# Fused linear attention and gated FFN: seven block products for tiles 8 and 9 of the down projection, tile 10 in their banks, and no forced query unit

## The chip, the cores and the metric

The kernel runs on one core of one Trainium2 chip. The metric is the device time of one execution in microseconds (us), the median of several runs. PE is the matmul engine (TensorE), DVE, ACT and POOL are VectorE, ScalarE and GpSimd, SP is the engine whose queue issues nearly all of the DMAs.

## The reference

```python
xn = layernorm(x)                            # x: 2048 x 512
q, k, v = heads(xn @ wqkv)                   # 32 heads of 16
phi_q = [softmax(q @ w_phi), softmax(-(q @ w_phi))]      # phi_k the same way
kv, z = phi_k.T @ v, phi_k.sum(tokens)       # per head
o = (phi_q @ kv) / (phi_q @ z + 1e-6)
s = o @ wo
h = relu(xn @ W_gate) * (xn @ W_up)          # 2048 x 1376
out = x + s * silu(h @ W_down)
```

All is float32.

## The kernel before

**Precision.** Each operand is split into a high part (rounded for the fast matmul) and a low part (the remainder). A product is three matmuls into one bank: low weight x high data, high weight x low data, high x high (`mm3`, or `mm` three times). A split is a copy to the high part on ACT and a subtraction on POOL or DVE for the low part (`split`). Names: hh, hl are the high and low part of the FFN's hidden values, fdh, fdl of the down weights of a tile, wth, wtl of a weight block that is loaded for a block product, XT slots are reused for operands of block products.

**Tiling.** Tokens are 4 blocks of 512. Half 0 is blocks 0 and 1 (b0, b1), half 1 is blocks 2 and 3. The 1376 hidden features are 11 tiles of 128, of which the last is part full. For each tile `gate_up` makes gate and up of both blocks of a half by a seven-product scheme in four banks pa, pb, pc, pd; it is a generator that yields between products, and other work (the down products of earlier tiles, query projections) is put in at the yields. Its last two steps finish the hidden values of b1 (t7) and b0 (r).

**The down projection.** In half 0 tiles go in chunks, and the chunk (8, 9, 10) comes after the last `gate_up`: b1's products, then b0's, each ended by a Silu. In half 1, the down products of tiles 0 to 3 (group 0) and 4 to 7 (group 1) are made transposed (features on partitions) as 7 block products in place of 8. `operand_parts` makes the sums of hidden values on POOL and splits them, `weight_sums` makes those of the down weights on POOL and puts them into DRAM tiles wdt{g}{i}{h,l} (group g, product i), `weights` loads them back as wth, wtl, and `turned_down(g)` issues the matmuls, product i in the order of ORDER, two tiles t each, two feature tiles k deep. Products 1, 2 and 4 take a weight block as it is. The products of one bank are added up there, and DVE adds the bank to y. Tiles 8, 9 and 10 (REST_F) are made plainly in `last_turned`, 2 blocks x 4 columns of 128 x 3 tiles x 3 matmuls. Then comes `out_turned` (pso: the attention output times wo, 12 matmuls a bank, times y, plus x) for two pairs of query tiles, and the last ones in `out_tile`.

**Queries.** The features of queries are made in units of two (`q_pair`: exponentials, row sums, normalization eq), and `q_back` is a unit's back part: DVE transposes eq to ez, 32 small matmuls (pnum) multiply it with the key-value state, and ACT copies the numerators out, to be stored to DRAM (od). They are read back as `of` and split to oh, ol for pso.

**What sets the order.** All operations are recorded in the order in which the program issues them (`InOrder`, so that nearly all have one line in the profile: L75), and each engine keeps that order. The program order itself comes from a planner: the class `Clock` holds rough costs, and at each `pump` a background generator goes on as soon as its inputs are there by that clock and its engine's backlog is within a limit; `finish` runs one to its end at once. `weight_sums`, `weights`, `operand_parts` and the queries are such generators. SP's queue issues its DMAs in order.

Of the kernel before, what the change touches and what calls it, by code (L numbers as in the profile page):

```python
# [8 lines left out]
F32R = mybir.dt.float32r  # L9
AF = mybir.ActivationFunctionType  # L10
ALU = mybir.AluOpType
# [38 lines left out]

GROUPS = [(0, 1, 2, 3), (4, 5, 6, 7)]
IN_GROUP = {f: (g, m // 2, m % 2) for g, fs in enumerate(GROUPS) for m, f in enumerate(fs)}
ORDER = (5, 3, 1, 6, 7, 2, 4)
PLAIN = {1: (0, 0), 2: (0, 1), 4: (1, 1)}
# [121 lines left out]
def layer_kernel(ctx: ExitStack, tc: tile.TileContext, x, wkT, wqT, wv, wo, wf, cst, out):  # L176
# [539 lines left out]
    def d_load(g):  # L716
        RD[g] = [u4((P, 2, D), "rd") for h in range(2)]
        for m, f in enumerate(GROUPS[g]):
            nc.sync.dma_start(RD[g][m // 2][:, m % 2, :], wf[f][:, 1024:])

    WDT = {(g, i): [dram((P, 512), f"wdt{g}{i}{x}") for x in "hl"] for g in range(len(GROUPS)) for i in (5, 6, 3, 7)}

    def weight_sums():

        for g in range(len(GROUPS)):
            if g not in RD:
                yield 100,
                d_load(g)
            a11, a21, a12, a22 = (halves(t)[:, x] for t in RD.pop(g) for x in range(2))
            yield 40,  # L730
            yield "sync", a11, a22
            t = u2((P, 8, 64), "ds")
            for i in (5, 6, 3, 7):
                a, b, op = {5: (a21, a22, ALU.add), 6: (t, a11, ALU.subtract), 3: (a12, t, ALU.subtract),
                            7: (a11, a21, ALU.subtract)}[i]
                yield "gpsimd", a, b
                add(nc.gpsimd, t, a, b, op)
                parts = [u2((P, 2, 8, 32), f"dt{x}", F32R) for x in "hl"]
                hi, lo = (x.rearrange("p t k j -> p k t j") for x in parts)
                src = t.rearrange("p k (t j) -> p k t j", t=2)  # L740
                yield "sync", t
                yield "scalar", t
                nc.scalar.activation(hi, src, AF.Copy)
                yield "gpsimd", hi
                add(nc.gpsimd, lo, src, f32(hi), ALU.subtract)

                def put(parts=parts, g=g, i=i):
                    for x, d in zip(parts, WDT[g, i]):
                        nc.sync.dma_start(d, f32(x).rearrange("p t k j -> p (t k j)"))
                    SUMMED.add((g, i))  # L750
                PUTS[g, i] = pace.when(parts[1], put)
                del parts, hi, lo, src, a, b, put
            del t, a11, a21, a12, a22
        yield None,

    def weights():

        for g in range(len(GROUPS)):
            for i in ORDER:
                while len(AW) > DEEP or i not in PLAIN and (g, i) not in SUMMED:  # L760
                    yield 2,
                if i in PLAIN:
                    n, m = PLAIN[i]
                    AW[i] = [u2((P, 2, 2, P), f"wt{x}", F32R) for x in "hl"]
                    for k in range(2):
                        for x, w in enumerate(AW[i]):
                            nc.sync.dma_start(f32(w[:, k]).rearrange("p t c -> p (t c)"),
                                              wspill[GROUPS[g][2 * m + k]][7 + x][:, 256 * n:256 * n + 256])
                else:
                    yield "sync", *WDT[g, i]  # L770
                    AW[i] = [u2((P, 2, 8, 32), f"wt{x}", F32R) for x in "hl"]
                    for w, d in zip(AW[i], WDT[g, i]):
                        nc.sync.dma_start(f32(w).rearrange("p t k j -> p (t k j)"), d)
                MADE.add((g, i))
        yield None,
# [21 lines left out]

    def gate_up(f, used, halfway, whole=False):

# [33 lines left out]
        used(A22)  # L833
        nc.vector.scalar_tensor_tensor(t7, pb, 0.0, t7, op0=ALU.max, op1=ALU.mult)
        if whole:
            h1 = t7
            raised(f, h1)
        else:
            h1 = u2((P, BT), "hh", F32R), u2((P, BT), "hl", F32R)
            split(*h1, t7, nc.gpsimd)  # L840
        yield
        mm3(pd, w_of(f, 3), a_of(S4), range(2), first=False)
        used(S4)
        add(nc.vector, r, pd, r, ALU.mult)
        if whole:
            LATE.append(lambda: lowered(f, r))
        else:
            h0 = u2((P, BT), "hh", F32R), u2((P, BT), "hl", F32R)
            LATE.append(lambda: split(*h0, r, nc.gpsimd))
            HS[f] = [h0, h1]  # L850
        FT.pop(f)
        yield

    def gate_up_apart(f, used, halfway, whole=False):

# [68 lines left out]
    def operand_parts():  # L924
# [14 lines left out]
        needs = {5: (0, 0), 3: (2, 1), 1: (0, 0), 6: (2, 1), 7: (2, 1), 2: (2, 0), 4: (2, 0)}  # L939
        drops = {1: (0, 0), 7: (0, 1)}  # L940
        for g in range(len(GROUPS)):
            for i in ORDER:
                ops, ts = [], []
                for k in range(2):
                    while (g, *needs[i], k) not in B:
                        yield 1,
                    t, a, b = made(g, i, k)
                    if a is not None:
                        yield "sync", a, b
                        yield "gpsimd", a, b  # L950
                        add(nc.gpsimd, t, a, b, ALU.subtract)
                    ts.append(t)
                    t = a = b = None
                while len(OPS) > 1:
                    yield 1,
                for k in range(2):
                    t = ts.pop(0)
                    if i in (3, 6, 2):
                        hi, lo = (XT[:, A21, s, k, :] for s in range(2))
                    else:  # L960
# [6 lines left out]
                    ops.append((hi, lo))  # L967
                    del t, hi, lo
                if i in drops:
                    for k in range(2):  # L970
                        B.pop((g, *drops[i], k))
                if i == 4:
                    for k in range(2):
                        B.pop((g, 5, k)), B.pop((g, 2, 0, k)), B.pop((g, 2, 1, k))
# [4 lines left out]
    def turned_down(g):  # L979
# [5 lines left out]
        def out(i, t):  # L985
            return Y[b1 if i in (3, 6, 5, 7) else b0][:, t + (2 if i in (5, 7, 4) else 0), :]
        held = {}
        for i in ORDER:
            pace.finish(operands, lambda: (g, i) in READY)
# [4 lines left out]
            for t in range(2):  # L994
                c = {5: "y", 3: "y", 2: "z"}.get(i, "x"), t
                first = c not in held
                if first:
# [4 lines left out]
                                  for x in (wh, wl)],  # L1002
                    lambda k: OPS[i][k], range(2), first)
                del wh, wl
                if t == 1:
                    del AW[i], OPS[i]
                y = out(i, t)
                if g or i in (6, 7, 2):
                    add(nc.vector, y, p, y)
# [4 lines left out]
                del p  # L1014
                yield

    def last_split():
# [258 lines left out]
    def last_turned():  # L1276

        for j in (1, 0):
            b = (b0, b1)[j]
            if j == 0:  # L1280
                o_split_turned(0)
                o_load_turned(1)
            parts = {}
            first, last = REST_F[:-1], REST_F[-1:]

            def rows(d, fs, start, stop):
                if start:
                    parts[d] = ps(name="py")
                for m, f in enumerate(fs):
                    (hh, hl), (dh, dl) = HS[f][j], [t[:, d * P:d * P + P] for t in WD[f]]  # L1290
                    mm(parts[d], dl, hh, start and m == 0, False)
                    mm(parts[d], dh, hl, False, False)
                    mm(parts[d], dh, hh, False, stop and m == len(fs) - 1)
                pace.pump()
            if j:
                for d in range(3):
                    rows(d, first, True, False)
            for d in range(4):
                if d in parts:
                    rows(d, last, False, True)  # L1300
                else:
                    rows(d, REST_F, True, True)
                y = Y[b][:, d, :]
                add(nc.vector, y, parts[d], y)
                nc.scalar.activation(y, y, AF.Silu)
        for f in REST_F:
# [517 lines left out]
    for half in range(2):  # L1824
# [7 lines left out]
        for f in range(NF):  # L1832
# [30 lines left out]
            def halfway():  # L1863
                if again:
                    f_reload(f + 1, 2 if half and f + 1 in IN_GROUP else 1)
            run((gate_up if pending or half and f > 1 else gate_up_apart)(f, used, halfway, whole),
                dict.fromkeys(STEPS_AT.get(f, ()), 1) if half else DOWNS)
            if half:
                for g, fs in enumerate(GROUPS):
                    if f == fs[2]:  # L1870
# [15 lines left out]
        for j, b in enumerate((b1, b0)):  # L1886
            j = 1 - j
            if b == b0:
                pace.finish(queries)
                pace.finish(BACK[Q_UNITS[0][1] - 1])  # L1890
                for q in QUERIES[half][:2]:
# [90 lines left out]
```

## Time and profile before

| | |
|---|---|
| median of 3 runs | 541.59 us (540.87 to 541.63) |
| the profiled execution | 540.95 us, span 539.2 us, granted clock 1.000 |
| instructions | 9274 |
| busy: PE, POOL, DVE, ACT | 532.7, 403.9, 381.0, 258.7 us |
| DMA | 136.48 MB, mean 253 GB/s |

The span goes from the first to the last instruction. Busy times are summed by engine. Matmuls are pipelined: one is shown with 0.39 us, while they start 0.23 us apart. In a row "out<-in" are the tiles written and read, then partitions x elements and the count; in square brackets stands the idle time of the engine ahead of the row, and what ended it.

### The profile page before, as it was taken

The numbers are of one execution on the slowest core, as the hardware profiler recorded it, in microseconds if no ns is written. First come the engines' busy times: TensorE is split into PE (matmuls) and PEld (weight loads), VectorE is DVE, ScalarE is ACT, GpSimd is POOL, SyncE is SP. The second block draws the span as 40 slices with busy tenths as digits, with TensorE's granted clock in tenths as the row PEclk, the third lists the DMA queues.
The fourth block names the chain that finished last, engine by engine and source line by source line (L and its number), as shares of the span: only waits on it lengthen the run. The fifth ranks groups of instructions, "written<-read, shape, count | busy, mean of one in ns | idle before, by whom it ended". The sixth has DMA issues, their size and how long they took to land.

```text
span 539.2 us, 9274 instructions
## 1 busy us (share of the span) xinstructions
PE 532.7 (99%) x3162; PEld 436.3 (81%) x3162; DVE 381.0 (71%) x614; ACT 258.7 (48%) x462; POOL 403.9 (75%) x353
## 2 busy tenths in 40 slices
PE   9999999999999999999999999999999999999996
PEld 8898887888887888787887868887887887878885
DVE  5988777688877338789898942888547758853475
ACT  3788767564524665545535251343644535335310
POOL 0669999867787999899898644693998976963560
PEclk9999999999999999999999999999999999999999
DMA  8439789647899857887869999798956895916754
GB/s 266 168 118 339 165 220 243 134 114 185 227 284 353 306 184 273 290 290 295 271 245 322 395 424 398 275 343 289 360 204 212 301 310 194 349 38 195 228 164 156
DMA packets 92111, 136.48 MB, mean 253 GB/s; under 512 B 8096, under 2 KB 43808, under 8 KB 91168
## 3 DMA queue, kind: packets, MB, share of 16 engines
q1 hardware_dynamic: 89904, 128.48, 69.1%
q0 software_dynamic: 2016, 7.34, 7.7%
q8 instruction: 25, 0.41, 0.3%
q14 instruction: 22, 0.18, 0.1%
q10 hardware_dynamic: 144, 0.07, 0.0%
HBM read 74.25 MB, written 57.41 MB: 244 GB/s over the span
## 4 chain that ended last, share of the span: by engine, by line
PE 85%; POOL 5%; ACT 4%; DVE 3%; issue 2%; POOLq 0%; DVEq 0%; ACTq 0%
PE py L75 21%; PE pd L75 12%; PE pa L75 12%; PE pb L75 10%; PE pso L75 8%; PE pc L75 7%; PE pk L75 6%; PE pq L75 3%; PE pv L75 2%; PE pnum L75 2%; POOL XT L75 1%; PE pkv L75 1%; POOL t L75 1%; ACT junk L75 1%; PE pidle L75 1%
## 5 line engine op out<-in xcount | busy, mean ns | idle before, releaser
L75 DVE TENSOR_TENSOR y<-py,y 128x512 f32<-128x512 f32 x60 | 41.1, 687 | 38.2 <-PE py L75 38.1
L75 PE MATMUL pa<-XT,wa 128*128 128x512 f32 x264 | 67.1, 390 | 0.0
L75 PEld LDWEIGHTS pa<-XT,wa 128*128 128x128 f32 x264 | 49.5, 188 | 10.7 <-issue 0.4
L75 POOL TENSOR_TENSOR ez<-eq,zB 128x1024 f32<-128x1024 f32 x16 | 38.4, 2410 | 0.0
L75 POOL TENSOR_TENSOR hl<-t,hh 128x512 fp32r<-128x512 f32 x21 | 27.1, 1297 | 13.2 <-ACT hh L75 10.9
L75 PE MATMUL py<-fdh,hl 128*128 128x512 f32 x88 | 34.5, 392 | 0.0
L75 POOL TENSOR_TENSOR ol<-of,oh 128x512 fp32r<-128x512 f32 (+1 forms) x14 | 19.9, 1453 | 19.4 <-ACT oh L75 16.3
L75 PE MATMUL py<-fdl,hh 128*128 128x512 f32 x88 | 34.2, 389 | 0.0
L75 PE MATMUL py<-fdh,hh 128*128 128x512 f32 x88 | 34.2, 389 | 0.0
L75 PE MATMUL pd<-XT,wc 128*128 128x512 f32 x132 | 34.1, 391 | 0.0
L75 PE MATMUL pd<-XT,wd 128*128 128x512 f32 x132 | 33.9, 391 | 0.0
L75 PE MATMUL pb<-XT,wb 128*128 128x512 f32 x132 | 33.6, 390 | 0.0
L75 PE MATMUL pc<-XT,wb 128*128 128x512 f32 x132 | 33.5, 389 | 0.0
L75 DVE TENSOR_TENSOR pb<-pb,t 128x512 f32<-128x512 f32 x17 | 11.9, 699 | 28.7 <-ACT pd L75 28.5
L75 PE MATMUL pq<-XT,wqh 128*128 128x512 f32 (+1 forms) x112 | 30.7, 360 | 0.0
L75 PE MATMUL pk<-wkh,XT 128*128 128x512 f32 x88 | 30.2, 395 | 0.0
L75 DVE TENSOR_REDUCE mx<-pk 128x32 f32<-128x512 f32 x32 | 20.4, 680 | 13.2 <-PE pk L75 13.2
L75 PEld LDWEIGHTS pd<-XT,wd 128*128 128x128 f32 x132 | 24.6, 188 | 5.8 <-issue 0.8
L75 PEld LDWEIGHTS pd<-XT,wc 128*128 128x128 f32 x132 | 24.6, 188 | 5.8 <-issue 0.8
L75 PEld LDWEIGHTS pb<-XT,wb 128*128 128x128 f32 x132 | 24.7, 188 | 5.5 <-issue 0.4
L75 PEld LDWEIGHTS pc<-XT,wb 128*128 128x128 f32 x132 | 24.8, 188 | 5.2
L75 ACT ACTIVATE pb<-pa 128x512 f32<-128x512 f32 x17 | 9.9, 583 | 33.6 <-PE pa L75 33.5
(243 smaller groups left out, 1600.4 us busy)
## 6 DMA issues: line engine op xcount, KB each, us to landing
xts<-XT SPq DMA_DIRECT2D x4, 1792.0 KB
zacc<-ek POOLq DMA_DIRECT2D x14, 512.0 KB, 5.4
XT<-xts SPq DMA_DIRECT2D x7, 1024.0 KB
rawg<-wf SPq DMA_DIRECT2D x22, 256.0 KB
ws<-wa SPq DMA_DIRECT2D x22, 256.0 KB
ws<-wb SPq DMA_DIRECT2D x22, 256.0 KB
ws<-wc SPq DMA_DIRECT2D x22, 256.0 KB
wa<-ws SPq DMA_DIRECT2D x22, 256.0 KB
```

The lines of the kernel that those rows point to most:

```text
L75: return self.tc.keep_in_program_order(op(*a, **k))
```

## The change

It has four parts.

1. Tiles 8 and 9 are a third group, one feature tile deep: seven products of 2 x 3 matmuls. Its sums of down weights are made before those of group 1 (the pause of 100 ahead of a group's loads is gone), from the raw weights of two more tiles. `last_turned` drives the products by `turned_down(2)`.
2. Tile 10 stays plain, and its products run into the banks of products 3, 2 and 4, and into a bank of its own after product 7 (`rest`). Its hidden values stay in their PSUM banks and are split by ACT and DVE, not POOL (`direct`).
3. `operand_parts` makes the operand sums of the next product ahead of the wait for a free place, for all groups.
4. In half 0, ahead of b0's last products, the back part of query unit 3 isn't brought to its end any more.

```diff
-GROUPS = [(0, 1, 2, 3), (4, 5, 6, 7)]
-ORDER = (5, 3, 1, 6, 7, 2, 4)
+GROUPS = [(0, 1, 2, 3), (4, 5, 6, 7), (8, 9)]
+DEPTH = [len(fs) // 2 for fs in GROUPS]
+HELD = [1, 1, 3]
+ORDERS = [(5, 3, 1, 6, 7, 2, 4), (5, 3, 1, 6, 7, 2, 4), (1, 5, 6, 3, 7, 2, 4)]
...
     def weight_sums():
-        for g in range(len(GROUPS)):
+        for g in (0, 2, 1):
+            if g == 1:
+                yield 0,
             if g not in RD:
-                yield 100,
                 d_load(g)
...
-    def gate_up(f, used, halfway, whole=False):
+    def gate_up(f, used, halfway, whole=False, direct=False):
...
-        nc.vector.scalar_tensor_tensor(t7, pb, 0.0, t7, op0=ALU.max, op1=ALU.mult)
+        alone = direct and not whole
+        h = pb if alone else t7
+        nc.vector.scalar_tensor_tensor(h, pb, 0.0, t7, op0=ALU.max, op1=ALU.mult)
...
-            split(*h1, t7, nc.gpsimd)
+            split(*h1, h, nc.vector if alone else nc.gpsimd)
...
     def operand_parts():
...
-            for i in ORDER:
...
+            for n, i in enumerate(order):
+                while not there(i):
+                    yield 1,
+                if i not in summed:
+                    yield from sums_for(i)
+                while len(OPS) > HELD[g] or DEPTH[g] == 1 and n in (1, 2) and 2 in OPS:
+                    yield 1,
+                if n + 1 < len(order) and (i, order[n + 1]) != (5, 6) and there(order[n + 1]):
+                    yield from sums_for(order[n + 1])
...
     def turned_down(g):
...
+        last = g == len(GROUPS) - 1
+        def rest(p, i, t):
+            b, d = i in (3, 7), t + (2 if i in (7, 4) else 0)
+            for f in REST_F:
+                (hh, hl), (dh, dl) = HS[f][b], [x[:, d * P:d * P + P] for x in WD[f]]
+                mm(p, dl, hh, i == 7 and f == REST_F[0], False)
+                mm(p, dh, hl, False, False)
+                mm(p, dh, hh, False, f == REST_F[-1])
...
+                if last and i in (3, 2, 4):
+                    rest(p, i, t)
                 if g or i in (6, 7, 2):
                     add(nc.vector, y, p, y)
...
+                if last and i == 7:
+                    p = ps(name="py")
+                    rest(p, i, t)
+                    add(nc.vector, y, p, y)
+                if last and i in (7, 3, 2, 4):
+                    nc.scalar.activation(y, y, AF.Silu)
+                    yield
...
     def last_turned():
-        for j in (1, 0):
...
+        n = 0
+        pending.append(turned_down(len(GROUPS) - 1))
+        for _ in pending.pop(0):
+            pace.pump()
+            n += 1
+            if n == 14:
                 o_split_turned(0)
                 o_load_turned(1)
...
                 pace.finish(queries)
-                pace.finish(BACK[Q_UNITS[0][1] - 1])
```

The new orders of the engines show where this lands. On PE in half 0, the query unit's pnum stands among the last products (py) before:

```order
L75 MATMUL py<-fdh,hh 128x512
L75 MATMUL pnum<-ez,kvt 32x256 x16
L75 MATMUL py<-fdh,hl 128x512
L75 MATMUL py<-fdl,hh 128x512
L75 MATMUL py<-fdh,hh 128x512
```

After, the same engine has it behind all of them, right ahead of pso:

```order
L77 MATMUL py<-fdh,hl 128x512
L77 MATMUL py<-fdl,hh 128x512
L77 MATMUL py<-fdh,hh 128x512
L77 MATMUL pnum<-ez,kvt 32x256 x16
L77 MATMUL pso<-woh,ol 128x512
L77 MATMUL pso<-wol,oh 128x512
```

36 products that stood behind pnum stand ahead of it now.

On PE at the end of half 1, the last plain products before and the first pso; each bank of py gets nine matmuls, three for each of three tiles:

```order
L75 MATMUL py<-hh,fdl 128x512
L75 MATMUL py<-hl,fdh 128x512
L75 MATMUL py<-hh,fdh 128x512
L75 MATMUL pso<-oh,wol 128x512
L75 MATMUL pso<-ol,woh 128x512
```

After, the same place has a block product of group 2 (its operand in an XT slot, wtl and wth the weights) and tile 10's three matmuls (fdl, fdh) into the same bank:

```order
L77 MATMUL py<-XT,wtl 128x512
L77 MATMUL py<-XT,wth 128x512 x2
L77 MATMUL py<-hh,fdl 128x512
L77 MATMUL py<-hl,fdh 128x512
L77 MATMUL py<-hh,fdh 128x512
L77 MATMUL pso<-oh,wol 128x512
```

Nine matmuls have become six here, and the first three need an operand that POOL makes.

On POOL, around the low part dtl of product 3's weights of group 1 (dtl_4718 here; hl are low parts of operands, ds the weight sums, ez a query unit's exponentials times the state's sums z, t1 operand sums):

```order
L75 TENSOR_TENSOR hl_4768<-t1_4188,hh_4767 128x512
L75 TENSOR_TENSOR hl_4772<-t1_4199,hh_4771 128x512
L75 TENSOR_TENSOR t1_4790<-t7_4465,r_4504 128x512
L75 TENSOR_TENSOR t1_4815<-t7_4613,r_4649 128x512
L75 TENSOR_TENSOR dtl_4718<-ds_4555,dth_4717 128x8x2x32
L75 TENSOR_TENSOR ds_4555<-rd_4471 128x512
```

After, the same piece is dtl_4898, and the weight sums of group 2 have all gone by ahead of it:

```order
L77 TENSOR_TENSOR dtl_4833<-ds_4693,dth_4832 128x8x2x32
L77 TENSOR_TENSOR ds_4693<-rd_4586,ds_4693 128x512
L77 TENSOR_TENSOR ez_4903<-eq_4738,zB_2243 128x1024
L77 TENSOR_TENSOR hl_4911<-t1_4855,hh_4910 128x512
L77 TENSOR_TENSOR hl_4939<-t1_4866,hh_4938 128x512
L77 TENSOR_TENSOR dtl_4898<-ds_4693,dth_4897 128x8x2x32
```

An ez and the two hl that followed the dtl before now stand ahead of it.

More of the change, by code (lines that the diff above doesn't have):

```diff
@@ L49 @@
 A21, A22, A11, A12, S3, S2, S1, S4 = range(8)
-GROUPS = [(0, 1, 2, 3), (4, 5, 6, 7)]
-IN_GROUP = {f: (g, m // 2, m % 2) for g, fs in enumerate(GROUPS) for m, f in enumerate(fs)}
-ORDER = (5, 3, 1, 6, 7, 2, 4)
+GROUPS = [(0, 1, 2, 3), (4, 5, 6, 7), (8, 9)]
+DEPTH = [len(fs) // 2 for fs in GROUPS]
+HELD = [1, 1, 3]
+IN_GROUP = {f: (g, *divmod(m, DEPTH[g])) for g, fs in enumerate(GROUPS) for m, f in enumerate(fs)}
+ORDERS = [(5, 3, 1, 6, 7, 2, 4), (5, 3, 1, 6, 7, 2, 4), (1, 5, 6, 3, 7, 2, 4)]
 PLAIN = {1: (0, 0), 2: (0, 1), 4: (1, 1)}
@@ L716, in d_load @@
     def d_load(g):
[L717 to L721, printed above, removed]
+        RD[g] = [(u4 if DEPTH[g] > 1 else u2)((P, DEPTH[g], D), "rd") for h in range(2)]
+        for f in GROUPS[g]:
+            _, h, k = IN_GROUP[f]
+            nc.sync.dma_start(RD[g][h][:, k, :], wf[f][:, 1024:])
+    WDT = {(g, i): [dram((P, 256 * DEPTH[g]), f"wdt{g}{i}{x}") for x in "hl"]
+           for g in range(len(GROUPS)) for i in (5, 6, 3, 7)}
     def weight_sums():
-        for g in range(len(GROUPS)):
+        for g in (0, 2, 1):
+            if g == 1:
+                yield 0,
             if g not in RD:
-                yield 100,
                 d_load(g)
@@ L731, in weight_sums @@
             yield "sync", a11, a22
-            t = u2((P, 8, 64), "ds")
+            t = u2((P, 4 * DEPTH[g], 64), "ds")
             for i in (5, 6, 3, 7):
@@ L737, in weight_sums @@
                 add(nc.gpsimd, t, a, b, op)
-                parts = [u2((P, 2, 8, 32), f"dt{x}", F32R) for x in "hl"]
+                parts = [u2((P, 2, 4 * DEPTH[g], 32), f"dt{x}", F32R) for x in "hl"]
                 hi, lo = (x.rearrange("p t k j -> p k t j") for x in parts)
@@ L758, in weights @@
         for g in range(len(GROUPS)):
-            for i in ORDER:
+            for i in ORDERS[g]:
                 while len(AW) > DEEP or i not in PLAIN and (g, i) not in SUMMED:
@@ L763, in weights @@
                     n, m = PLAIN[i]
-                    AW[i] = [u2((P, 2, 2, P), f"wt{x}", F32R) for x in "hl"]
-                    for k in range(2):
+                    AW[i] = [u2((P, DEPTH[g], 2, P), f"wt{x}", F32R) for x in "hl"]
+                    for k in range(DEPTH[g]):
                         for x, w in enumerate(AW[i]):
                             nc.sync.dma_start(f32(w[:, k]).rearrange("p t c -> p (t c)"),
-                                              wspill[GROUPS[g][2 * m + k]][7 + x][:, 256 * n:256 * n + 256])
+                                              wspill[GROUPS[g][DEPTH[g] * m + k]][7 + x][:, 256 * n:256 * n + 256])
                 else:
                     yield "sync", *WDT[g, i]
-                    AW[i] = [u2((P, 2, 8, 32), f"wt{x}", F32R) for x in "hl"]
+                    AW[i] = [u2((P, 2, 4 * DEPTH[g], 32), f"wt{x}", F32R) for x in "hl"]
                     for w, d in zip(AW[i], WDT[g, i]):
@@ L843, in gate_up @@
         used(S4)
-        add(nc.vector, r, pd, r, ALU.mult)
+        h = pd if alone else r
+        add(nc.vector, h, pd, r, ALU.mult)
         if whole:
@@ L848, in gate_up @@
             h0 = u2((P, BT), "hh", F32R), u2((P, BT), "hl", F32R)
-            LATE.append(lambda: split(*h0, r, nc.gpsimd))
+            LATE.append(lambda: split(*h0, h, nc.vector if alone else nc.gpsimd))
             HS[f] = [h0, h1]
@@ L852, in gate_up, with gate_up_apart @@
         yield
-    def gate_up_apart(f, used, halfway, whole=False):
+    def gate_up_apart(f, used, halfway, whole=False, direct=False):
         pa = ps(name="pa")
@@ L939, in operand_parts, with there, sums_for @@
         needs = {5: (0, 0), 3: (2, 1), 1: (0, 0), 6: (2, 1), 7: (2, 1), 2: (2, 0), 4: (2, 0)}
-        drops = {1: (0, 0), 7: (0, 1)}
+        drops = {7: (0, 1)}
         for g in range(len(GROUPS)):
[L942 to L946, printed above, removed]
+            ks, order, summed = range(DEPTH[g]), ORDERS[g], {}
+            def there(i):
+                return all((g, *needs[i], k) in B for k in ks)
+            def sums_for(i):
+                summed[i] = []
+                for k in ks:
                     t, a, b = made(g, i, k)
@@ L951, in operand_parts @@
                         add(nc.gpsimd, t, a, b, ALU.subtract)
-                    ts.append(t)
+                    summed[i].append(t)
                     t = a = b = None
-                while len(OPS) > 1:
+            for n, i in enumerate(order):
+                while not there(i):
                     yield 1,
-                for k in range(2):
+                if i not in summed:
[4 more added lines that the diff above has]
+                    yield from sums_for(order[n + 1])
+                ops, ts = [], summed[i]
+                for k in ks:
                     t = ts.pop(0)
-                    if i in (3, 6, 2):
-                        hi, lo = (XT[:, A21, s, k, :] for s in range(2))
+                    slot = k if DEPTH[g] > 1 else (n + 3) % 4
+                    if i in (3, 6, 2) if DEPTH[g] > 1 else slot < 2:
+                        hi, lo = (XT[:, A21, s, slot, :] for s in range(2))
                     else:
@@ L968, in operand_parts @@
                     del t, hi, lo
+                if n == 2:
+                    for k in ks:
+                        B.pop((g, 0, 0, k))
                 if i in drops:
-                    for k in range(2):
+                    for k in ks:
                         B.pop((g, *drops[i], k))
                 if i == 4:
-                    for k in range(2):
+                    for k in ks:
                         B.pop((g, 5, k)), B.pop((g, 2, 0, k)), B.pop((g, 2, 1, k))
@@ L986, in out @@
             return Y[b1 if i in (3, 6, 5, 7) else b0][:, t + (2 if i in (5, 7, 4) else 0), :]
+        last = g == len(GROUPS) - 1
         held = {}
-        for i in ORDER:
+        def rest(p, i, t):
[5 more added lines that the diff above has]
+                mm(p, dh, hh, False, f == REST_F[-1])
+        for i in ORDERS[g]:
             pace.finish(operands, lambda: (g, i) in READY)
@@ L1002, in turned_down @@
                                   for x in (wh, wl)],
-                    lambda k: OPS[i][k], range(2), first)
+                    lambda k: OPS[i][k], range(DEPTH[g]), first)
                 del wh, wl
@@ L1015, in turned_down @@
                 yield
+                if last and i == 7:
[5 more added lines that the diff above has]
+                    yield
+                p = None
     def last_split():
@@ L1276, in last_turned @@
     def last_turned():
-        for j in (1, 0):
-            b = (b0, b1)[j]
-            if j == 0:
+        n = 0
[4 more added lines that the diff above has]
+            if n == 14:
                 o_split_turned(0)
                 o_load_turned(1)
[L1283 to L1305, printed above, removed]
         for f in REST_F:
@@ L1865, in halfway @@
                     f_reload(f + 1, 2 if half and f + 1 in IN_GROUP else 1)
-            run((gate_up if pending or half and f > 1 else gate_up_apart)(f, used, halfway, whole),
+            run((gate_up if pending or half and f > 1 else gate_up_apart)(f, used, halfway, whole, half == 1),
                 dict.fromkeys(STEPS_AT.get(f, ()), 1) if half else DOWNS)
             if half:
-                for g, fs in enumerate(GROUPS):
+                for g, fs in enumerate(GROUPS[:-1]):
                     if f == fs[2]:
```

## The prediction

> **What bounds the kernel now.** I read the page's head and its busy times first, then its chain by engine, then the waits of PE, then the chain in order of time. From the page:
>
> ```profile
> span 539.2 us, 9274 instructions
> ...
> PE 532.7 (99%) x3162; PEld 436.3 (81%) x3162; DVE 381.0 (71%) x614; ACT 258.7 (48%) x462; POOL 403.9 (75%) x353
> ...
> PE 85%; POOL 5%; ACT 4%; DVE 3%; issue 2%; POOLq 0%; DVEq 0%; ACTq 0%
> ```
>
> PE (TensorE) is busy for 532.7 of 539.2 us and makes up 85% of the chain. All that PE waits for, past the fill of the first microseconds:
>
> ```profile
> PE pidle L75 <- DVE mhalf L75: 1.1, 1, 1.1
> PE pnum L75 <- DVE ez L75: 0.8, 1, 0.8
> PE pk L75 <- ACT pk L75: 0.2, 1, 0.2
> ```
>
> So a change gains only by matmuls that PE no longer issues, or by the 0.8 us at pnum. It loses by anything that comes too late for PE. The rows of the chain in time (start, length) around the two places that the change touches:
>
> ```profile
> 307.88 8.17 PE py L75 x36
> ...
> 318.68 8.41 PE py L75 x36
> 327.09 10.88 PE pso L75 x48
> ...
> 484.38 17.69 PE py L75 x78
> 502.08 32.80 PE pso L75 x156
> ```
>
> The last gives the price of a 512-column matmul in a stream: 78 in 17.69 us, 0.2268 us each. At 484 PE does the last products of half 1: 6 that still belong to group 1, and 72 of tiles 8, 9 and 10.
>
> **Term 1: six matmuls fewer.** Before: 2 blocks x 4 columns of 128 x 3 tiles x 3 = 72. After: tiles 8 and 9 as seven products of 2 x 3 matmuls = 42, tile 10 in 2 x 4 x 3 = 24, together 66. The last product of group 1 keeps its 6. So 78 becomes 72, and pso starts 6 x 0.2268 = **1.36 us** earlier, if each operand is there in time. The Trainium skill ("TensorE: Matmul & The Clock Gate", Back-to-back issue gap) gives 216 ns for a single 512-column matmul and 131 ns for a sustained stream; by the first, as an estimate, the six would be worth 1.29 us, by the second 0.79. The row above (226.8 ns over 78) speaks for the first and against the second.
>
> **Term 2: no forced query unit in half 0.** Before, the back part of query unit 3 is brought to its end ahead of b0's products, so that its pnum matmuls stand in the middle of the y additions on which DVE is busy. PE and then DVE there:
>
> ```profile
> 315.65 0.39 PE L75 MATMUL py<-fdh,hh 128*128 128x512 f32 x1
> 315.97 0.66 PE L75 MATMUL pnum<-ez,kvt 64*32 64x256 f32 x16
> 317.44 1.25 PE L75 MATMUL pnum<-ez,kvt 64*32 64x256 f32 x16 [0.81 <-DVE ez L75]
> 318.61 0.50 PE L75 MATMUL py<-fdh,hl 128*128 128x512 f32 x1
> ```
>
> ```profile
> 316.07 0.69 DVE L75 TENSOR_TENSOR y<-py,y 128x512 f32<-128x512 f32 x1 [1.35 <-PE py L75]
> 316.68 1.29 DVE L75 STREAM_TRANSPOSE ez<-eq 128x512 f32<-128x512 f32 x2
> ```
>
> PE's last matmul of b1 takes its place until 315.65 + 0.23 = 315.88, and pso begins at 327.09: 11.21 us. The 36 products between take 8.17 (the row at 307.88), so pnum with its wait costs 3.04. The same 32 pnum matmuls, undisturbed, in half 1:
>
> ```profile
> 481.63 0.84 PE L75 MATMUL pd<-XT,wd 128*128 128x512 f32 x3
> 482.40 1.09 PE L75 MATMUL pnum<-ez,kvt 64*32 64x256 f32 x32
> 483.42 0.96 PE L75 MATMUL pd<-XT,wd 128*128 128x512 f32 x3
> 484.22 0.40 PE L75 MATMUL py<-hh,wtl 128*128 128x512 f32 x1
> ```
>
> From 481.63 to 484.22 are 2.59 us; six pd matmuls take 1.36, so pnum costs 1.23. After, pnum stands behind the 36 products and right ahead of pso. Its two transposes follow the same y addition and end some 2.1 us after it starts, while pnum is issued up to 8.2 us later than now: no wait. Gain 3.04 - 1.23 = **1.82 us**. The lower bound is the wait alone, 0.81; the rest is switching between kinds of matmul in the middle of a wait, and could come back in part at the new place. I take 1.82, since the undisturbed row has such switches too. What pnum feeds (its normalization, then the store of that unit's numerators) comes later; the loads of it for half 0's outputs stand behind stores that wait for the last Silu of y anyway, so I cost that at nothing. If the cover goes, pso of half 0 is late.
>
> **What is added, and what hides it.** Rows of POOL and ACT by kind, of the stretch with groups 0 to 2, and of POOL near the end:
>
> ```profile
> L75 POOL TENSOR_TENSOR XT<-t,XT 128x512 fp32r<-128x512 f32 x8 | 10.3, 1309 | 11.9 <-ACT XT L75 11.9
> L75 POOL TENSOR_TENSOR hl<-t,hh 128x512 fp32r<-128x512 f32 x21 | 27.1, 1297 | 13.2 <-ACT hh L75 10.9 <-PE py L75 2.1
> L75 POOL TENSOR_TENSOR t<-t,t 128x512 f32<-128x512 f32 x6 | 7.7, 1305 | 0.0
> L75 POOL TENSOR_TENSOR wa<-rawg,wa 128x256 fp32r<-128x256 f32 x22 | 16.1, 768 | 0.0
> L75 POOL TENSOR_TENSOR ez<-eq,zB 128x1024 f32<-128x1024 f32 x16 | 38.4, 2410 | 0.0
> ...
> L75 ACT ACTIVATE hh<-t 128x512 fp32r<-128x512 f32 x21 | 12.9, 629 | 23.8 <-DVE t L75 19.2 <-DMA of<-od 3.3 <-DMA ws<-wc 1.3
> ```
>
> ```profile
> core 0: us, PE busy (x) PEld busy (x) DVE busy (x) ACT busy (x) POOL busy (x), PEclk, DMA share, GB/s
> 375.00:485.00 110.00, 110.00 (x567) 89.20 (x566) 74.58 (x112) 49.99 (x85) 92.65 (x65) 1.00 0.71 244
> 485.00:503.00 18.00, 18.00 (x81) 14.92 (x80) 6.37 (x10) 8.48 (x14) 6.36 (x5) 1.00 0.60 182
> ```
>
> POOL gets 7 low parts (1.30) and 4 operand sums (1.305) for group 2, 14.3 us, and loses 6 low parts of tiles 8, 9 and 10, 7.8. Group 2's weight sums and their low parts add 8 operations of 256 columns; the nearest row of that size is wa, 0.77, so 6.2. Together 12.7 us more, against 17.4 idle of 110 and 11.6 idle of 18. It fits as a sum, so the order decides. ACT gets 7 high parts of 0.63 and loses 4, beside 60 us idle. DVE gets two low parts of tile 10 and 8 more y additions, 10 x 0.69 = 6.9, most of it in the 18 us in which it is busy for 6.4. The DMAs added (raw rows of two tiles, weight sums out and in) are some 2.5 MB, in a stretch whose queues are 71% busy.
>
> **The order at the end.** I set zero at the end of the last gate/up product (484.22 now). Tile 10's last pb then ends at -2.72, twelve slots of 0.227 ahead. Its DVE product (0.69, 0.19 later) ends at -1.84, ACT's hh of it at -1.1 and the high part of product 6 behind it at -0.4. From there POOL does the low part of product 6, the sum for 7 and the low part of 3: -0.4 + 1.31 + 1.31 + 1.30 = 3.5. PE does product 3 after four products of 1.36, at 5.44, and reads the low part one slot later, 5.67: 2.1 us to spare. Products 7, 2 and 4 follow at distances of 2.72 on PE, and have over 3. Then pso, at 72 x 0.2268 = 16.3:
>
> ```profile
> 490.55 2.05 DVE L75 TENSOR_TENSOR y<-py,y 128x512 f32<-128x512 f32 x3 [4.07 <-PE py L75]
> ...
> 494.68 0.63 ACT L75 ACTIVATE y<-y 128x512 f32<-128x512 f32 x1 [1.41 <-DVE y L75]
> 495.22 2.18 ACT L75 ACTIVATE oh<-of 128x512 fp32r<-128x512 f32 x4
> ...
> 495.91 5.06 POOL L75 TENSOR_TENSOR ol<-of,oh 128x512 fp32r<-128x512 f32 x4 [8.64 <-ACT oh L75]
> ```
>
> After, b1's last y is at 10.88 on PE, its Silu ends at 10.88 + 0.19 + 0.69 + 0.63 = 12.4, the first ol starts 0.69 later at 13.0, and the fourth ends 5.06 on, 18.1. PE wants the fourth at 16.3 + three groups of 0.68 + 0.23 = 18.6. 0.5 us to spare, where now there are 3.4 (500.97 against 502.08 + 2.27). This is the tightest place. I cost it at nothing, bounds 0 and 1.
>
> **The order at group 1's weights.** POOL, then SP, then PE:
>
> ```profile
> 419.46 1.30 POOL L75 TENSOR_TENSOR dtl<-ds,dth 128x512 fp32r<-128x512 f32 x1
> ```
>
> ```profile
> 420.27 0.43 SPq L75 DMA_DIRECT2D wdt13h<-dth  x1
> ...
> 423.94 1.31 SPq L75 DMA_DIRECT2D wth<-wdt13h  x1
> ```
>
> ```profile
> 440.94 0.39 PE L75 MATMUL py<-XT,wtl 128*128 128x512 f32 x1
> ```
>
> Group 1's weight sums come behind group 2's now. Ahead of the dtl at 419.46 POOL has 11.2 us more to do: the 8 small operations (6.2), two hl (2.6) and one ez (2.4) that the order puts there. The idle time that it can fill on the way is 3 to 8 us, so dtl comes 3 to 11 us later; I take 8, since most of POOL's idle there is waits for PE that stay. Then dtl ends at 428.8, and store to load (420.27 to 423.94, 3.67) and the same again to land bring the weights at 436.2. PE wants them at 440.94 - 1.82 = 439.1. 2.9 us to spare; with all 11.2 in the way, 0.3 too late. By the Trainium skill ("DMA: Bandwidth & Descriptors", Anatomy of one DMA), 2 us and a share by bytes, 256 KB would land in about 2.6 us, an estimate for GpSimd's path; each trip would then be a microsecond shorter than the row has it.
>
> **Sum.** -1.36 - 1.82 = -3.18, all else hidden. The profiled execution took 540.95 (span 539.2 and 1.75 around it), so 537.8. It lies 0.64 under the median of 541.59; against the median the forecast is **538.4**.
>
> **Rivals.**
> 1. Group 1's weights come late (slower). The place is product 3 of group 1, the price is the lateness itself, since PE does nothing else meanwhile. Past 3.2 us, that is dtl some 14 us later than now, the kernel is slower than before; 5 us late gives 543.4. For it: a queue of DMAs in order on SP, in which one late store holds those behind. Against: POOL's load there grows by 11.2 at most. Chance 0.06.
> 2. The operands of the end come late: the fourth ol (0.5 to spare), or product 3's low part (2.1). A stall of 1 to 2 us leaves 539.4 to 540.4. For it: the chain runs over DVE, ACT and POOL, each step with a release that I put at 0.1 to 0.2. Against: POOL is idle before 10 and after 5 there. Chance 0.2.
> 3. Half 0 gives only the wait: -1.36 - 0.81, 539.4; chance 0.12. If the unit is still waited for, at its new place, the removal doesn't do what it says: -1.36 alone, 540.2; chance 0.1. Against it: 8 us of slack.
>
> My forecast has 0.5; 0.02 is left for a wait that I don't see. The difference that a measurement of this kernel can tell is about 0.2%, 1.1 us; below 540.5 is faster. Faster: 0.5 + 0.12, nearly all of rival 2 and most of the 0.1, 0.85. Same 0.09, slower 0.06. The range goes from 537.6 (the forecast less the 0.8 by which the three runs of before lie apart, 540.87 to 541.63) to 540.5, which takes in rivals 2 and 3 and leaves out rival 1 and the largest stalls.
>
> **What would show it.** PE's waits: the row pnum <- DVE ez gone, and no new row of py or pso. The chain: py x72 in 16.3 us ahead of the pso x156. pso of half 0 at 325.3 in place of 327.1, on the same span from its start. POOL's dtl of wdt13 near 428, and the first matmul of group 1's product 3 without an idle time. I am wrong if a py waits for XT or wth, or pso for ol.

## The result and the profile after

The changed kernel takes 537.37 us (median of 4 runs, 537.11 to 537.61), the kernel before 541.36 (4 runs, 540.87 to 541.63): ratio 0.9927, interval 0.991 to 0.9944, or 3.0 to 4.9 us less. The forecast was 538.4, 3.2 less. The sign was right; the time lies 0.2 under the lower end of the range, 537.6. The page after, its head and busy times, then PE's waits and the chain in time:

```profile
span 535.3 us, 9349 instructions
...
PE 530.0 (99%) x3156; PEld 434.6 (81%) x3156; DVE 388.0 (72%) x624; ACT 261.2 (49%) x469; POOL 415.6 (78%) x366
```

```profile
PE pidle L77 <- DVE mhalf L77: 1.1, 1, 1.1
PE pxT L77 <- DVE xt L77: 0.3, 1, 0.3
PE pk L77 <- ACT pk L77: 0.2, 1, 0.2
```

```profile
307.65 16.32 PE py L77 x72
325.00 11.10 PE pso L77 x48
...
482.53 16.32 PE py L77 x72
498.85 32.80 PE pso L77 x156
```

PE issues six matmuls fewer, POOL is busy for 11.7 us more, and the wait at pnum is gone, as the prediction had it. No new wait took its place (pxT is in the first 6 us and comes and goes with the first loads). Half 0's 72 products now run in one piece, with pnum behind them:

```profile
323.59 0.39 PE L77 MATMUL py<-fdh,hh 128*128 128x512 f32 x1
323.90 1.09 PE L77 MATMUL pnum<-ez,kvt 64*32 64x256 f32 x32
324.93 0.50 PE L77 MATMUL pso<-woh,ol 128*128 128x512 f32 x1
```

The last place where the two spans part is behind the last matmul. DVE's last operation, before and then after:

```profile
535.36 0.42 DVE L75 TENSOR_TENSOR sx<-yk,sx 128x256 f32<-128x256 f32 x1
```

```profile
532.13 0.42 DVE L77 TENSOR_TENSOR sx<-yk,sx 128x256 f32<-128x256 f32 x1
```

From there to the end of the span it is 539.2 - 535.78 = 3.4 us before and 535.3 - 532.55 = 2.8 after. Cut at the same events, the profiled executions compare like this:

| stretch | before | after | difference |
|---|---|---|---|
| start to half 0's last products | 307.88 | 307.65 | -0.23 |
| from there to the end of half 0's pso | 30.09 | 28.45 | -1.64 |
| to the last products of half 1 | 146.41 | 146.43 | +0.02 |
| to the last matmul | 50.50 | 49.12 | -1.38 |
| last matmul to the landing of the last store | 2.64 | 2.66 | +0.02 |
| landing to the end of the span | 1.66 | 1.02 | -0.64 |

The landings are the last semaphore updates by the DMAs in the traces (537.52 and 534.31). The traces' semaphore instructions tell what the last row is. A lane is here one of eight semaphores on which SP's DMAs report that they have landed; the DMAs take them in turn. After its last DMA, SP waits for each of the eight lanes in a fixed order, the first lane first, about 0.06 us each, and only then do all engines end. The last store is on the second lane before, with six lanes still to be waited for; after, with 20 DMAs more, it is on the sixth, with two to go. That is four waits, some 0.25 us. Most of the rest is a gap of 0.37 in place of 0.06 between two of these waits, which the trace of after doesn't have. A DMA for instructions begins 0.64 us behind that gap, and there is none at the end after. It is this row of the window from 525 to 541 us of before:

```profile
q14 instruction: 1, 0.01, 0.2%
```

### The profile page after: what moved, and what is told of

Read it like the earlier page. It is cut to its first block, busy times and chain, and to the rows that moved or that the text cites. A ratio compares the mean times of both kernels' runs of the same rounds, so it can differ in the third digit from the quotient of the medians.

```text
span 535.3 us, 9349 instructions
## 1 busy us (share of the span) xinstructions
PE 530.0 (99%) x3156; PEld 434.6 (81%) x3156; DVE 388.0 (72%) x624; ACT 261.2 (49%) x469; POOL 415.6 (78%) x366
## 4 chain that ended last, share of the span: by engine, by line
PE 84%; POOL 5%; ACT 4%; DVE 3%; issue 1%; DMA 1%; POOLq 0%; DVEq 0%; ACTq 0%
PE py L77 21%; PE pa L77 12%; PE pd L77 12%; PE pb L77 10%; PE pso L77 8%; PE pc L77 7%; PE pk L77 6%; PE pq L77 3%; PE pv L77 2%; PE pnum L77 2%; POOL XT L77 1%; PE pkv L77 1%; POOL t L77 1%; ACT junk L77 1%; POOL xf L77 1%
## 5 line engine op out<-in xcount | busy, mean ns | idle before, releaser
L77 DVE TENSOR_TENSOR y<-py,y 128x512 f32<-128x512 f32 x68 | 46.1, 686 | 24.3 <-PE py L77 24.1
L77 POOL TENSOR_TENSOR hl<-t,hh 128x512 fp32r<-128x512 f32 x20 | 25.7, 1294 | 9.5 <-ACT hh L77 9.3
```

The costliest lines, as they stand in the source:

```text
L77: return self.tc.keep_in_program_order(op(*a, **k))
```

## The experiments

**Part 4 alone.** One line is taken out of the kernel before.

```diff
-                pace.finish(BACK[Q_UNITS[0][1] - 1])
```

> The kernel before with part 4 alone: the query unit is no longer forced in half 0. Theory: pnum with its wait costs 2.89 us where it stands (the 11.05 us from the last place of b1's products to the last place of b0's, less 36 products of 0.2268) and 1.24 behind the products, so half 0 ends 1.64 us earlier, nothing else moves, and the time is about 1.6 us less (ratio 0.997). Rival: only the wait of 0.81 goes, ratio 0.9985. The end of the program after the last store's landing stays at 1.7 us as before.

Measured: 539.38 us, before 541.01, ratio 0.9967 (0.9954 to 0.9979), 1.63 less. The chain in time:

```profile
308.09 16.32 PE py L75 x72
325.44 11.10 PE pso L75 x48
482.96 17.69 PE py L75 x78
```

Half 0 is as in the changed kernel (16.32, 11.10), while the end of half 1 still has 78 matmuls. From the start of half 0's products to the end of pso it is 28.45, against 30.09 in the kernel before. So the 1.64 us come from this line, and they are more than the wait of 0.81. The end after the landing is 1.66, as before.

**The lanes.** Some loads of wo in half 0 are cut into two halves: four in the kernel before, four and two in the changed one. The bytes and all else stay.

```diff
+                parts = 2 if s == 0 and k < cut else 1
+                for c in range(parts):
+                    x_ = slice(c * D // parts, (c + 1) * D // parts)
-                nc.sync.dma_start(f32(t[k][s]), wos[s][k])
+                    nc.sync.dma_start(f32(t[k][s])[:, x_], wos[s][k][:, x_])
```

> The kernel before, with four of the loads of wo in half 0 cut into two halves, so that four DMAs more are issued, the same bytes. Theory of the lanes: SP ends the program by waiting for its eight DMA lanes in a fixed order, about 0.065 us each; the last store then is on the sixth lane, as in the changed kernel, and not on the second; four waits fewer stand behind its landing: 0.25 us less, and with the 0.37 us break in that row of waits gone too, 0.6 us (1.0 from the last landing to the end in place of 1.7). Rival, chance: the end of a program varies by half a microsecond from execution to execution, and this one is as before, 1.7 or anything between. The rest of the span stays within 0.2 us.

> The changed kernel with the same four more DMAs; the last store moves from the sixth lane to the second. Theory of the lanes: 0.25 us more from its landing to the end (1.25 in place of 1.0), and up to 1.7 if the break of 0.37 comes with the place of the waits. Chance: no relation, about 1.0. Against the kernel before 3.2 to 3.7 us less.

> The changed kernel with two more DMAs, the last store on the last lane. Theory of the lanes: two waits fewer behind its landing than in the changed kernel, 0.13 us less, 0.85 from the landing to the end. Chance: no relation. Against the kernel before about 4.0 to 4.1 us less.

Measured, with the end after the last landing in the profiled execution:

| kernel | last store on lane | landing to end, us | time, us | ratio to before (interval) |
|---|---|---|---|---|
| before | 2 | 1.66 | 541.01 | |
| before, 4 more | 6 | 1.04 | 540.47 | 0.9985 (0.9976 to 0.9994) |
| changed | 6 | 1.02 | 537.37 | 0.9927 (0.991 to 0.9944), to 541.36 |
| changed, 4 more | 2 | 1.27 | 537.76 | 0.994 (0.9926 to 0.9953) |
| changed, 2 more | 8 | 0.90 | 537.20 | 0.9923 (0.991 to 0.9937) |

The end follows the lane in all three, within 0.05 of what was expected. Four DMAs more, for the same bytes, make the kernel before 0.54 us faster. The changed kernel with four and with two more is 3.25 and 3.81 us faster than the kernel before (expected 3.2 to 3.7 and 4.0 to 4.1). Against the changed kernel itself these are 0.39 more and 0.17 less, which goes the way of the lanes, but the medians are from different series. The gap of 0.37 isn't tied to the lane: the changed kernel with four more has the second lane without it. It stands in all three profiles that have an instruction DMA at the end (before, part 4 alone, before with four more), 0.63 to 0.64 us ahead of that DMA each time, and in none of the seven others. In the kernel before with four more it falls between the waits for the first two lanes and ends at 536.92, while the last store lands at 537.75, so that it costs nothing there. That the gap is the fetch of those instructions is likely, and was not tried by itself.

**Part 3 undone.** An operand's sum is made only when its product's place is free.

```diff
-                if n + 1 < len(order) and (i, order[n + 1]) != (5, 6) and there(order[n + 1]):
-                    yield from sums_for(order[n + 1])
```

> The changed kernel without part 3: an operand's sum is made only when its product has a free place. The number of matmuls, and their order at the end, are those of the changed kernel; POOL's low part of product 4 of group 2 now stands behind the four ol that wait for b1's last Silu. Theory: order on POOL decides there; the four ol end at 18.2 us after the last gate/up product, the low part 1.3 later at 19.5, PE wants it at 13.8, so PE waits about 5.5 us at product 4 and the time is about 542.9 us, slower than before by 1.5. Rival, only the amount of work on POOL counts: POOL is idle for several microseconds there, so the time stays within 0.3 us of the changed kernel, 537.4.

Measured: 545.07 us against 540.97, ratio 1.0075 (1.0062 to 1.0088). PE at product 4 of group 2:

```profile
498.54 0.50 PE L77 MATMUL py<-XT,wtl 128*128 128x512 f32 x1 [2.52 <-ACT XT L77]
501.68 1.22 PE L77 MATMUL py<-XT,wth 128*128 128x512 f32 x2 [2.64 <-POOL XT L77]
502.70 0.63 PE L77 MATMUL py<-hh,fdl 128*128 128x512 f32 x1
503.13 0.63 PE L77 MATMUL py<-hl,fdh 128*128 128x512 f32 x1
...
506.02 0.39 PE L77 MATMUL py<-hh,fdh 128*128 128x512 f32 x1
```

The wait is where the theory puts it, in two pieces, for ACT's high part and for POOL's low part, 5.2 us together (expected 5.5). The same matmuls with another order on POOL and ACT lose more than the change gains. But the time is 2.2 above the expected 542.9: behind the waits the matmuls start 0.43 us apart in place of 0.227, for some ten of them. The trace has the granted clock at 0.50 from 499.07 to 505.90, and PE has work in the 4.2 us from 501.68 on; half of that is 2.1 us.

**Tile 10's low parts on POOL.**

```diff
-            run((gate_up if pending or half and f > 1 else gate_up_apart)(f, used, halfway, whole, half == 1),
+            run((gate_up if pending or half and f > 1 else gate_up_apart)(f, used, halfway, whole, False),
```

> The changed kernel with tile 10's low parts made by POOL again, not DVE. Theory: two more operations of 1.3 us stand ahead of product 3's low part on POOL, which would end 5.2 us after the last gate/up product in place of 3.2, where PE wants it at 5.7: still 0.4 to spare, so no wait and the same time within 0.2 us, 537.4. Rival: the slack is less than I think, PE waits up to 1 us at product 3, 538.4, and the rest behind it is moved as well.

Measured: 537.51 us, ratio 0.9939 (0.9927 to 0.995). POOL, and PE at product 3:

```profile
484.32 1.29 POOL L77 TENSOR_TENSOR XT<-t,XT 128x512 fp32r<-128x512 f32 x1
...
488.08 2.54 POOL L77 TENSOR_TENSOR hl<-t,hh 128x512 fp32r<-128x512 f32 x2
```

```profile
489.58 0.39 PE L77 MATMUL py<-hh,wtl 128*128 128x512 f32 x1
489.81 0.39 PE L77 MATMUL py<-hl,wth 128*128 128x512 f32 x1
```

Product 3's low part ends at about 489.35 (the first of the two) and is read at 489.81: 0.45 to spare, as expected, and no wait. So that piece of the change gains nothing that could be seen here. (This profiled execution was 1.8 us late already at half 0's products, 309.43, with 0.8 of it a wait for the first weights.)

**Weight sums in the order of the groups.**

```diff
-        for g in (0, 2, 1):
-            if g == 1:
-                yield 0,
+        for g in range(3):
```

> The changed kernel with the weight sums made for the groups in the order 0, 1, 2, without the pause of zero. Theory: the weights of product 3 of group 1 have 4.6 us to spare in the changed kernel (wtl lands at 434.4, PE wants it at 439.1), so their earlier making gains nothing, and group 2's, which come later now, are wanted only 45 us behind: the same time within 0.2 us, 537.4. Rival: group 1's weights were near the limit on SP's queue and something else gains, or group 2's loads come late at the end, each a few tenths.

Measured: 538.71 us, ratio 0.9964 (0.9951 to 0.9977), 1.3 slower than the changed kernel. Neither the theory nor the rival came out. SP, POOL and PE:

```profile
423.10 0.60 SPq L77 DMA_DIRECT2D wdt26h<-dth  x1
```

```profile
429.54 0.74 POOL L77 TENSOR_TENSOR dtl<-ds,dth 128x256 fp32r<-128x256 f32 x1 [5.96 <-DMA wdt26h<-dth]
...
431.05 2.40 POOL L77 TENSOR_TENSOR ez<-eq,zB 128x1024 f32<-128x1024 f32 x1
```

```profile
435.36 1.66 PE L77 MATMUL pd<-XT,wd 128*128 128x512 f32 x6 [1.11 <-DVE t L77]
```

POOL stands for 6 us ahead of a dtl until the store of an earlier weight sum, issued at 423.10, is done; the ez behind it comes late, DVE's row sum waits for that ez, DVE's addition stands behind the row sum, and PE waits 1.1. No weights came late for PE: a small operation on POOL waited, and the operations behind it on POOL were wanted.

**Group 1's weights late.** The pause ahead of group 1's weight sums is 100 units in place of 40.

```diff
-            yield 40,
+            yield 100 if g == 1 else 40,
```

> The changed kernel with the weight sums of group 1 held back by 60 units of the planner (a pause of 100 in place of 40). PE's order is the same. On POOL an ez, an eq and two low parts, 7.0 us, now stand ahead of the low part dtl of product 3's weights. Theory of rival 1: lateness turns into PE time one for one behind the slack of 4.6 us; dtl ends near 435.5, its store and load take 3.1 and 2.7 or more, so the weights are there at 442, PE waits some 3 us (2 to 5) at group 1's product 3, and the time is about 540.4. If PE's wait is caught up again later (other theory), the time stays below 538.

Measured: 543.90 us (expected 540.4), ratio 1.0053 (1.004 to 1.0066), 6.5 more than the changed kernel. PE, then a view by stretches (PE, PEld, DVE, ACT, POOL busy, the granted clock, the DMA share, GB/s):

```profile
444.55 0.77 PE L77 MATMUL py<-XT,wtl 128*128 128x512 f32 x1 [4.43 <-DMA wtl<-wdt13l]
```

```profile
444.00:448.00 4.00, 3.45 (x9) 2.79 (x10) 0.51 (x1) 0.00 (x0) 4.00 (x4) 0.57 0.94 271
448.00:452.00 4.00, 4.00 (x19) 3.29 (x18) 2.65 (x6) 2.16 (x4) 3.62 (x4) 1.00 0.82 290
```

The mechanism of rival 1 is there when it is forced: product 3 of group 1 waits for wtl, 4.4 us (expected 3, between 2 and 5). The dtl ends at 439.5 and not at 435.5. The price isn't the lateness alone. The order on PE is the same as in the changed kernel, so the two traces can be laid side by side, matmul by matmul. Behind the wait this run loses another 1.5 us. The trace has the granted clock at 0.50 from 443.99 to 447.40, PE has work in the 2.85 us from 444.55 on, and half of that is 1.4. (The rest of the 6.5 is 0.4 at 434.4, ahead of the wait, where the same pd as in the last run stands late, and 0.2 of the wait that the bracket doesn't show.) The Trainium skill ("TensorE: Matmul & The Clock Gate", What's actually happening) has the clock halved after an idle window of 3.4 us, and full again after as long a busy one. This run agrees in the main: a wait of 4.4 us, then the half clock for 3.4 us, though PE was busy only in the last 2.85 of these. In the run without part 3, two waits of 2.5 and 2.6 with one matmul between them did it too, each under 3.4.

## Why the prediction was right or wrong

**Six matmuls fewer: right.** Forecast -1.36, in the trace -1.38. The py x72 take 16.32 us, where 16.3 was forecast.

**The query unit: the mechanism right, the term too large.** Forecast -1.82; the trace has -1.64 and the line alone 1.63. The 3.04 us for pnum and its wait was mis-sized by 0.16. I began the distance at 315.88, a place of 0.23 us behind the start of b1's last matmul, and ended it at 327.09, where the chain has pso. But 327.09 is the end of the last py as shown, 0.39 us behind its start. The timeline of before:

```profile
326.70 0.39 PE L75 MATMUL py<-fdh,hh 128*128 128x512 f32 x1
326.93 0.39 PE L75 MATMUL pso<-woh,ol 128*128 128x512 f32 x1
```

By places of 0.23 us the py end at 326.93, and pso starts right there; the switch from py to pso costs nothing. With 11.05 in place of 11.21 the price is 2.89, less 1.24 behind the products: 1.64. (The two transposes end 1.9 us after the y addition starts, not 2.1; nothing hangs on that.) Rival 3, only the wait, is refuted by the run with part 4 alone.

**What I costed at nothing: right, and the places were the right ones.** In the changed kernel:

```profile
481.77 1.29 POOL L77 TENSOR_TENSOR XT<-t,XT 128x512 fp32r<-128x512 f32 x1 [1.90 <-ACT XT L77]
...
484.28 2.55 POOL L77 TENSOR_TENSOR hl<-t,hh 128x512 fp32r<-128x512 f32 x2
...
491.32 1.29 POOL L77 TENSOR_TENSOR XT<-t,XT 128x512 fp32r<-128x512 f32 x1 [1.99 <-ACT XT L77]
...
495.55 5.06 POOL L77 TENSOR_TENSOR ol<-of,oh 128x512 fp32r<-128x512 f32 x4 [2.94 <-ACT oh L77]
```

```profile
488.03 0.39 PE L77 MATMUL py<-hl,wth 128*128 128x512 f32 x1
...
498.69 0.39 PE L77 MATMUL pso<-oh,wol 128*128 128x512 f32 x1
```

With zero at 482.37, the start of group 1's last product, product 3's low part ends at about 485.55, 3.2 (forecast 3.5), and is read at 488.03. The fourth ol ends at 500.61, 18.2 (forecast 18.1); PE wants it at 498.69 + 3 x 0.68 + 0.23 = 500.96, so 0.35 is to spare where I had 0.5. Between them, product 4's low part ends at 492.61 and is read at 496.19, 3.6 later; that is the operand which the run without part 3 makes behind the four ol. And at group 1's weights:

```profile
427.24 1.30 POOL L77 TENSOR_TENSOR dtl<-ds,dth 128x512 fp32r<-128x512 f32 x1
```

```profile
431.73 0.32 SPq L77 DMA_DIRECT2D wtl<-wdt13l  x1
```

```profile
439.07 0.39 PE L77 MATMUL py<-XT,wtl 128*128 128x512 f32 x1
```

dtl ends at 428.5 (forecast 428.8). The store took 3.1 us and the load 2.7 by the DMA records, so wtl lands at 434.4, and 4.6 us are to spare (forecast 2.9). Rival 1 didn't come about; rival 2 didn't either.

**The sum: wrong by a term that it lacked, and by the time it was taken from.** The step "all else hidden" put what stands behind the last store at nothing, without a reason. I held the end of the program fixed, while 20 more DMAs moved the last store by four lanes: -0.64 in the traces, of which four lanes are 0.25 (1.27 against 1.02 in the changed kernel with and without four DMAs more) and the gap most of the rest; the kernel before gains 0.54 when only its DMAs are more. With it the sum is -1.38 - 1.64 - 0.64 = -3.66 in place of -3.18. That both lane and gap went the good way was luck: nothing in the change aimed at them.

The other step is the last one, from 537.8 to 538.4. The median of three runs, 541.59, lay 0.64 above the profiled execution, and I took the median. In the series of 15 and 17 runs behind the experiments the kernel before has 541.01 and 540.97, as the profiled one. 541.0 - 3.66 is 537.3; measured were 537.37. So of the miss of 1.0 about 0.5 is the sum and 0.6 the median of few runs. With either one of the two right, the same range around the forecast would have held the result. What stays unforeseen is the start: the first 300 us differ by 1.9 from execution to execution (307.55 to 309.43 to half 0's last products, of kernels that are the same up to there but for cut loads).

**Rival 1's price: wrong in size.** I gave lateness one for one. Where the wait was forced, the half clock behind it added 1.5 us, and 2.1 in the run without part 3.

## What to carry to other kernels

Where PE is 99% busy, compare each operation's end with the place where PE reads its result. This told the waits at the end of the kernel to a few tenths (5.2 us for 5.5, and none with 0.45 to spare), while the shares of busy time told nothing: the same work in another order on POOL cost 7.7 us. It was weaker where a queue of DMAs stood between (4.4 for 3), and it missed the 1.1 us of the other weight order. Measure a removed piece between the same kinds of event in both orders, starts to starts, so that the shown tail of a matmul isn't counted as gain. And look at what stands behind the last store: the number of DMAs, modulo the lanes, is part of the time.

## What the runs showed of the hardware

- The program's end waits for the eight DMA lanes in order, about 0.06 us each. The landing-to-end time went from 0.90 (last lane) over 1.02 to 1.04 (sixth) to 1.27 (second) with nothing but DMAs cut in two, and to 1.66 with a gap of 0.37 in the waits.
- A wait of 4.4 us on PE brought 3.4 us of half clock (matmuls 0.43 us apart); two waits of 2.5 and 2.6 us with one matmul between them brought 6.8. One of 1.1 us (the weight order) or 0.8 (before) brought none.
- A store of 128 KB from 128 partitions that was issued at 423.10 held its buffer until 429.4, 6.3 us. The DMA engines were busy for 0.92 of the time from 423 to 426.
